# An attention backward loop reordered: two written lists for PE and ACT, six dS buffers, smaller stores and loads

## The chip, the cores and the metric

The kernel runs on 1 core of one Trainium2 chip. The metric is the device time of one execution in microseconds (us). Every kernel was executed several times; the times below are medians. "PE" is the matmul engine, "ACT" the scalar engine, "DVE" the vector engine, "POOL" the general one; "SP" only issues DMA here.

## The reference, cut to what matters

One transformer block with adaptive layer norm, forward and the gradients of all inputs. Sequence 2048, width 512, 32 heads of 16, squared-ReLU MLP of 1792; inputs and outputs are bf16.

```
h   = layernorm(x) * (1 + ca) + sa
qkv = (h @ wqkv) split into q, k, v of 32 heads of 16
p   = softmax(q k^T / 4);   x = x + ga * (p v) @ wo
h   = layernorm(x) * (1 + cb) + sb
x   = x + gb * (relu(h @ w1 + b1)^2 @ w2 + b2)
out, vjp = jax.vjp(block, all inputs);   return out, *vjp(grad_out)
```

Everything below concerns one stage: the gradient of the attention. For each head it recomputes E = exp(scores), forms dS = E * dP, and from E and dS the gradients dV, dK and dQ.

## The kernel before: the parts that matter

The backward loop takes half of the time. Its unit is 4 heads x 128 queries x 512 keys; 4 units are a *block* (16 score matmuls, 8 DVE multiplies), 128 blocks in all, 16 for each group of 4 heads. The softmax's row terms ride in extra rows of q and dO, so that a plain multiply yields dS. For each unit:

```python
PE.matmul(psS, q, k)                        # 4 scores, one PSUM bank each
ACT.activation(E_u[:, hq], psS, Exp)        # 4 exponentials of 128x512
PE.matmul(psD, do, v)                       # 2 pairs of dP, two banks each
DVE.tensor_tensor(dS_u, psD, E_u, mult)     # 2 multiplies of 128x1024
SP.dma_start(dsT[:, qi], dS_u, transpose=True)      # 512 KB
PE.matmul(accVK, qz, dS_u); PE.matmul(accVK, dOs_tok, E_u)  # 2 "quads": dK and dV
```

dQ needs dS transposed. Seven of every eight units are transposed by DMA; the last unit of every second block is transposed on PE in two halves, and ACT evicts each half (`ptT`, 128x1024):

```python
def on_pe(b):
    return b % 2 == 1
def pe_turn(b, half):
    pt = psx.tile([P, 8, P], BF, name="ptT", tag="px")
    for i in range(8):
        PE.transpose(pt[:, i, :], held["dS"][...], identb[:])
    held["turn"] = (dst, pt)          # ACT evicts it in the next step
```

So the loop repeats every **pair of blocks**: one block that carries the two PE transpositions, one plain block. There are 64 pairs. The loop uses eight banks of PSUM, the memory that matmuls write: 4 for dP, 2 for scores, 1 for accVK, and one shared bank `px`, used in turn by some scores, by `ptT` and by the dQ product `dqacc`. E_u and dS_u have four buffers each. One loop over half units emits everything; a score and its exponential are written together:

```python
for j in range(2 * NU + 15):
    for hi in range(2):
        score(u, 2 * pair + hi, shared)      # matmul, then ACT.activation(Exp)
    if "turn" in held: ACT.activation(dst, pt[:], AF.Identity)
    dp_pair(...)                              # dP matmuls, DVE multiply, transposition
    (k_quad if pair == 0 else v_quad)(u - 2)
    if sub in (1, 3) and on_pe(b): pe_turn(b, sub // 2)
    if sub in (5, 6): dq_quad(...)            # dQ of the block before, then its eviction
    ...                                       # loads of the next heads, stores
```

## Time and profile before

| | before |
|---|---|
| median of 3 runs | 2,754.34 us (2,746.58 to 2,755.13) |
| span of the profiled run | 2,744.2 us |
| backward loop | about 1,270 to 2,620 us |
| mean length of a pair of blocks | 20.70 us |

The page's table of groups gives, for each line of the kernel: busy time and mean ns of one, then the engine's idle time before these instructions, and what ended most of it. Two of its lines for the kernel before:

```profile
L1058 DVE TENSOR_TENSOR dS_u<-psD_u,E_u 128x1024 bf16<-128x1024 f32 x1024 | 1196.4, 1217 | 146.8 <-PE psD_u L1056 88.9
...
L1116 PE MATMUL dqacc<-dsT,KS_tok 128*32 128x512 bf16 x2048 | 159.8, 390 | 12.2 <-ACT dsT L1157 12.2
```

DVE needs 1,196 us for its 1,024 multiplies and stands idle 147 us between them: no more than that can be won before DVE is full. The table of stretches for the loop's steady part has busy time and count of each engine, the mean granted clock of PE, the time of the DMA packets as a share of 16 engines' time (1.10 in the line below, so packets overlap), and GB/s:

```profile
core 0: us, PE busy (x) PEld busy (x) DVE busy (x) ACT busy (x) POOL busy (x), PEclk, DMA share, GB/s
1300.00:2560.00 1260.00, 1129.46 (x10664) 384.08 (x10660) 1133.25 (x970) 1180.72 (x2213) 130.98 (x95) 0.98 1.10 191
```

PE, DVE and ACT are each busy 90 to 94%; none is full. The clock of PE is nearly always full (0.98). The list of waits for the same stretch (engine and line, what it waited for, us in total, times, longest) says what separates them:

```profile
DVE dS_u L1058 <- PE psD_u L1056: 70.4, 125, 1.6
PE psS_u L1044 <- ACT E_u L1046: 60.4, 182, 1.1
ACT E_u L1046 <- PE psD_u L1056: 51.1, 80, 4.0
...
DVE dS_u L1058 <- DMA dsT<-dS_u: 16.7, 22, 3.5
```

DVE waits for dP, PE for a score bank that an exponential still holds, ACT for PE, and DVE for a dS buffer that a transposition still reads. The timeline of DVE over a pair (start, duration; in brackets the idle time before and who ended it) shows where: in the pair shown three times, 0.2 to 0.7 us each, around the transposing block.

```profile
2225.83 16.51 DVE L1058 TENSOR_TENSOR dS_u<-psD_u,E_u 128x1024 bf16<-128x1024 f32 x14 [0.61 <-PE psD_u L1056]
2243.03 1.23 DVE L1058 TENSOR_TENSOR dS_u<-psD_u,E_u 128x1024 bf16<-128x1024 f32 x1 [0.69 <-ACT vkb L1101]
2244.49 1.22 DVE L1058 TENSOR_TENSOR dS_u<-psD_u,E_u 128x1024 bf16<-128x1024 f32 x1 [0.23 <-PE psD_u L1056]
2246.40 16.51 DVE L1058 TENSOR_TENSOR dS_u<-psD_u,E_u 128x1024 bf16<-128x1024 f32 x14 [0.69 <-PE psD_u L1056]
```

From 2225.83 to 2246.40 is one pair: 20.57 us.

### The profile page before, as it was taken

To read this page: it belongs to the slowest core of one execution; us is meant where nothing else is said; L and a number is where in the kernel's file an instruction comes from. 1 tells how busy PE (TensorE), PEld (TensorE's weight loads), DVE (VectorE), ACT (ScalarE), POOL (GpSimd) and SP (SyncE) were. 2 spreads that over 40 slices of the span, in tenths; PEclk is the share of its full clock that TensorE was granted. 3 is DMA by queue.
4 is the path that set the end of the run, shared out by engine and by line. 5 is a ranking of instruction groups with operands and counts; after the bars stand their busy time and mean duration, and the time that the engine had idled before them with its cause. 6 is when DMAs were issued, how large, how long until landed. Compare 5 with 4: busy or idle time off the path is not lost.

```text
span 2744.2 us, 48487 instructions
## 1 busy us (share of the span) xinstructions
PE 2383.2 (87%) x18010; PEld 781.8 (28%) x18010; DVE 1763.4 (64%) x2232; ACT 2304.7 (84%) x3537; POOL 379.1 (14%) x378
## 2 busy tenths in 40 slices
PE   6799989888988988586898988988888989888899
PEld 2211123222322222232332333333233232332343
DVE  7101144435345443356988989989999898998973
ACT  4599999999999998202999999999999899998953
POOL 2000010211333133201011110101101011010100
PEclk8655569998998999787999999999999999999999
DMA  9863365346847656786999999999999999999982
GB/s 241 197 177 92 102 147 132 107 116 142 116 83 161 139 95 138 170 226 161 187 179 195 192 194 192 192 195 188 196 193 189 189 190 193 188 188 206 184 247 81
DMA packets 1271906, 459.69 MB, mean 168 GB/s; under 512 B 1152739, under 2 KB 1240807, under 8 KB 1271414
## 3 DMA queue, kind: packets, MB, share of 16 engines
q1 hardware_dynamic: 1254262, 425.42, 77.6%
q0 software_dynamic: 10944, 16.78, 4.2%
q10 hardware_dynamic: 6464, 14.40, 1.9%
q8 instruction: 142, 2.33, 0.3%
q14 instruction: 94, 0.77, 0.1%
HBM read 97.67 MB, written 74.47 MB: 63 GB/s over the span
## 4 chain that ended last, share of the span: by engine, by line
PE 27%; ACT 20%; DMA 4%; DVE 3%; issue 3%; SPq 1%; ACTq 1%; POOL 0%; DVEq 0%; POOLq 0%
ACT E_u L1046 15%; PE psS_u L1044 10%; PE accVK L1098 3%; ACT dsT L1157 3%; PE accVK L1089 3%; DVE dS_u L1058 2%; PE ptT L1079 2%; PE dqacc L1116 2%; PE pdh L1284 2%; PE pwq L1318 2%; DMA dsT<-dS_u 1%; PE psS_x L1044 1%; ACT dqtmp L1126 1%; PE psD_u L1056 1%; DMA part<-p_st 1%
## 5 line engine op out<-in xcount | busy, mean ns | idle before, releaser
L1058 DVE TENSOR_TENSOR dS_u<-psD_u,E_u 128x1024 bf16<-128x1024 f32 x1024 | 1196.4, 1217 | 146.8 <-PE psD_u L1056 88.9
L1046 ACT ACTIVATE E_u<-psS_u 128x512 bf16<-128x512 f32 x1790 | 990.8, 619 | 102.9 <-PE psD_u L1056 53.6
L701 ACT ACTIVATE ET<-psST 128x1024 bf16<-128x1024 f32 x1024 | 944.4, 1299 | 38.7 <-PE psST L699 37.7
L1044 PE MATMUL psS_u<-ik,iq 32*128 32x512 bf16 x1790 | 618.0, 386 | 106.2 <-ACT E_u L1046 64.7
L699 PE MATMUL psST<-qt_sb,kt_sb 32*128 32x512 bf16 x2048 | 408.3, 464 | 64.9 <-ACT ET L701 31.2
L1056 PE MATMUL psD_u<-iv,ido 32*128 32x512 bf16 x2048 | 406.6, 393 | 20.1 <-DMA ido<-dOT_st 14.3
L715 PE MATMUL oacc<-ET,vaug 128*32 128x512 bf16 x2048 | 247.5, 474 | 6.0 <-DVE ostage L719 6.0
L1044 PEld LDWEIGHTS <-iq 32*128 32x128 bf16 x2048 | 121.0, 91 | 342.2 <-issue 315.8
L1089 PE MATMUL accVK<-dS_u,qz 128*32 128x512 bf16 x2048 | 209.6, 398 | 3.0 <-DVE dS_u L1058 0.2
L1098 PE MATMUL accVK<-E_u,dOs_tok 128*16 128x512 bf16 x2048 | 205.4, 391 | 0.0
L699 PEld LDWEIGHTS <-kt_sb 32*128 32x128 bf16 x2048 | 90.0, 94 | 399.7 <-issue 388.6
L1131 POOL TENSOR_TENSOR dQacc<-dQacc,dqtmp 128x512 f32<-128x512 f32 x64 | 81.1, 1268 | 884.6 <-ACT dqtmp L1126 876.8
L1056 PEld LDWEIGHTS <-ido 32*128 32x128 bf16 x2048 | 105.1, 91 | 265.4 <-issue 262.4
L1046 ACT ACTIVATE E_u<-psS_x 128x512 bf16<-128x512 f32 x258 | 160.0, 620 | 14.8 <-PE psS_u L1044 14.6
L1116 PE MATMUL dqacc<-dsT,KS_tok 128*32 128x512 bf16 x2048 | 159.8, 390 | 12.2 <-ACT dsT L1157 12.2
L719 DVE COPY ostage<-oacc 128x512 f32<-128x512 f32 x32 | 22.0, 688 | 229.9 <-PE oacc L715 210.7
L376 DVE COPY part<-pm 128x512 f32<-128x512 f32 (+2 forms) x105 | 64.6, 615 | 150.7 <-PE pm L362 128.1
L1157 ACT ACTIVATE dsT<-ptT 128x1024 bf16<-128x1024 bf16 x128 | 134.4, 1050 | 1.1 <-PE ptT L1079 1.0
L715 PEld LDWEIGHTS <-vaug 128*32 128x32 bf16 x2048 | 54.9, 96 | 163.8 <-issue 163.8
L1044 PE MATMUL psS_x<-ik,iq 32*128 32x512 bf16 x258 | 100.4, 389 | 0.6 <-ACT E_u L1046 0.6
L1079 PE MATMUL ptT<-identb,dS_u 128*128 128x128 bf16 x1024 | 81.3, 224 | 11.6 <-ACT dsT L1157 11.4
L1089 PEld LDWEIGHTS <-qz 128*32 128x32 bf16 x2048 | 55.4, 93 | 123.3 <-issue 121.0
(262 smaller groups left out, 2104.1 us busy)
## 6 DMA issues: line engine op xcount, KB each, us to landing
p_st<-part POOLq DMA_DIRECT2D x36, 256.0 KB, 5.6
kt_sb<-qkT_st SPq DMA_DIRECT2D x128, 64.0 KB
wA<-in_B_w_dram SPq DMA_DIRECT2D x28, 256.0 KB
wB<-w1T_st SPq DMA_DIRECT2D x28, 256.0 KB
dsT<-dS_u SPq DMA_TRANSPOSE x448
wA<-w2T_st SPq DMA_DIRECT2D x21, 256.0 KB
wB<-in_B_w_dram SPq DMA_DIRECT2D x21, 256.0 KB
p_st<-part POOLq DMA_DIRECT2D x27, 192.0 KB, 4.2
```

The source lines that it names most:

```text
L699: PE.matmul(ps[:, hi, :], kt_sb[r:r + 32, kt * P:(kt + 1) * P], qt_sb[r:r + 32, :], start=True, stop=True, tile_position=(r, 0))
L701: ACT.activation(ET[:, 2 * pair:2 * pair + 2, :], ps[:], AF.Exp, scale=SCALE)
L715: PE.matmul(oacc[32 * hq:32 * hq + 32, :], lhsT, ET[:, hq, :], start=(kt == 0), stop=(kt == TT - 1), tile_position=(0, 32 * hq), skip_grou ...
L1044: PE.matmul(psS[:], st["q"][r:r + 32, qt * P:(qt + 1) * P], st["k"][r:r + 32, kc * 512:kc * 512 + 512], start=True, stop=True, tile_positi ...
L1046: ACT.activation(bst[u][0][:, hq, :], psS[:], AF.Exp, scale=SCALE)
L1056: PE.matmul(psD[:, hi, :], st["do"][r:r + 32, qt * P:(qt + 1) * P], st["v"][r:r + 32, kc * 512:kc * 512 + 512], start=True, stop=True, til ...
L1058: DVE.tensor_tensor(dS_u[:, 2 * pair:2 * pair + 2, :], psD[:], E_u[:, 2 * pair:2 * pair + 2, :], ALU.mult)
L1079: PE.transpose(pt[:, i, :], held["dS"][:, 2 * half + i // 4, kt * P:(kt + 1) * P], identb[:])
L1089: PE.matmul(cur["vk"][32 * hq:32 * hq + 32, :], hst[hg]["qz"][:, qt, hq, :], bst[u][1][:, hq, :], start=(qt == 0), stop=False, tile_positi ...
L1098: PE.matmul(acc[32 * hq:32 * hq + DH, :], dOs_tok[:, qt, (hg * 4 + hq) * DH:(hg * 4 + hq + 1) * DH], E_u[:, hq, :], start=False, stop=(qt ...
L1116: PE.matmul(acc[32 * hq:32 * hq + 32, :], KS_tok[:, kc * 4 + kt, h * DH:h * DH + 32], tT[:, :, hq * 4 + kt, :], start=(kt == 0), stop=(kt ...
L1157: ACT.activation(dst, pt[:], AF.Identity)
```

## The change

Its intent is to take the coupling losses out of the loop. The order of PE's and ACT's work is written as two lists, one for the block in which transpositions fall and one for the plain block; scores and exponentials are separate tokens and use three rotating banks A, B, C (C is `px`); dS has six buffers; the dK/dV store and the load of the q tokens are cut into quarters. No arithmetic changes.

```diff
-            yield hs["qs"][:], q_st[hg]
+            for i in range(4):
+                yield hs["qs"][:, 4 * i:4 * i + 4, :], q_st[hg][:, 4 * i:4 * i + 4, :]
...
-                at(j0 + 5 * i, load, to, fro)
+                at(j0 + 4 * i, load, to, fro)
...
+        banks = {"A": "ps0", "B": "ps1", "C": "px"}
...
+            if pair == 0:
+                bst[u][1] = ework.tile([P, 4, 512], BF, name="dS_u", tag="dS_u", bufs=6)
...
-                    if kc == QC - 1: ... at(cur["j"] + 4, load, dVKtP[hg], hst[hg]["vk"][:])
+                    part = slice(kc * 512, (kc + 1) * 512)
+                    at(cur["j"] + 4, load, dVKtP[hg][:, part], hst[hg]["vk"][:, part])
...
+        order_t = (
+            "s0 s1 q s2 e0 e1 D s3 D e2 s4 e3 t1 e4 q T1 D "
+            "s5 s6 e5 t2 e6 s7 T2 e7 D s8 e8 D s9 e9 q q s10 "
+            "s11 e10 D d1 d2 e11 Q q s12 D e12 s13 e13 q s14 D e14 "
+            "s15 q q e15 ").split(), "ABCABBABACABABCA"
+        order_n = (
+            "s0 D s1 q e0 q s2 e1 e2 D s3 s4 q s5 e3 D e4 "
+            "e5 s6 q s7 D s8 e6 e7 d1 e8 s9 D d2 e9 q Q s10 "
+            "s11 e10 D q s12 e11 e12 s13 e13 D q s14 s15 e14 e15 D q ").split(), "CBACBACBABABCABC"
...
-            for j in range(2 * NU + 15):
+            for b in range(NU // 4 + 3):
+                toks, bank = order_t if on_pe(b - 1) else order_n
+                for tok in toks: ...
```

In the lists `s` is a score matmul, `e` an exponential, `D` a pair of dP matmuls with its DVE multiply, `q` one quad for dK or dV, `t` a half of the PE transposition and `T` its eviction, `d` half of the dQ product and `Q` its eviction. The letters after each list are the banks of the 16 scores.

## The prediction

> **What bounds the kernel now.** The backward attention loop runs from 1,270 to 2,620 us, half of the 2,744 us span, and the change touches nothing else. It has 128 blocks (4 units of 4 heads), every second with a transposition on PE. The timeline repeats every pair of blocks: 20.3 to 20.6 us undisturbed, 1,327 us / 64 = 20.7 us on average. No engine is full. From 1,300 to 2,600 us, in the table of stretches, PE is busy about 90%, DVE 90%, ACT 94%, and the DMA engines hold transposes about 92% of the time.
>
> Floors per pair, from start-to-start pitches in the timeline:
> - DVE: 16 multiplies at 1.15 to 1.18 us: 18.4 to 18.9 us.
> - ACT: 32 exponentials at 0.475 us when nothing is missing (0.54 in the usual runs of four), two `ptT` evictions at 0.92, two dQ evictions at 0.475, half a `vkb`: about 18.2 us.[...]
> - PE: counting 0.32 us for each group that can run together (scores and dP in different row groups, quads, transposes), I estimate 18 to 18.5 us.
> - DMA: 7 transposes of 512 KB, 2.35 us each at the best 10 us of the trace, 2.6 to 2.7 over 20 to 30 us, plus loads and stores: 18 to 19 us.
>
> So four resources are near 18.5; about 2 us per pair are coupling losses. The list of waits (1,300 to 2,600) shows DVE idle 130 us: 73 for psD from PE, 17 behind `vkb` on ACT, 17 for dS buffers held by transposes. PE waits 62 for score banks held by exponentials.
>
> **What the change does.** No arithmetic goes. PE issues scores one by one instead of in pairs, three score banks rotate in a fixed list, evictions stand apart from the matmul that they follow, and the transposing block has its own list. ACT gets ahead in the plain block, behind in the other (8.1 and 9.9 us of ACT work against 9.3 of DVE). Six dS buffers (from four) remove most waits for transposes. The quarter stores and loads add 6 issues per head on ACT's queue[...] but split 512 KB bursts.
>
> **How much is critical.** The whole loop. I expect the DVE gaps to fall from 130 to about 50 us, and a pair to take 19.4 to 19.6 us: 64 x 1.2 = about 80 us less. Not more: all four then stand at 94 to 98%, and a faster loop pushes the transposes to their limit.
>
> **Predicted: 2,675 us**, 8 in 10 between 2,635 and 2,725. Faster by over 2%: 0.70; within 2%: 0.28; slower: 0.02.
>
> **What would show it.** Period of a pair of blocks 19.4 to 19.6 us; DVE busy 94 to 95% in the loop; waits of DVE for psD under 40 us and for dS transposes near zero; ACT's waits for PE about halved; durations, start and end unchanged.
>
> **What would make it wrong.** (a) DMA transposes turn out to be the wall: then DVE waits for dS buffers move later but remain, and the pair stays at 20 us or more. (b) A PE blocked at the head of its queue by a psD slot or the shared third bank, since single scores lose their concurrency. (c) More low-clock windows of PE. (d) The list is better than I think, and the pair reaches 18.7 us: 2,620 us.

The forecast's sum: 64 x 1.2, about 80 us off 2,754, hence 2,675. The pitches behind its floors are in the trace of the kernel before: at the least 1.13 us from one multiply to the next, 0.476 us from an exponential and 0.903 us from a `ptT` eviction to ACT's next instruction; and on PE two scores and a dP pair start within 0.02 us of 2227.71, the quad after them at 2228.04, the next scores 0.33 us later.

## The result and the profile after

| | before | after |
|---|---|---|
| median (4 runs each) | 2,753.24 us | 2,716.77 us |
| range | 2,746.58 to 2,755.13 | 2,708.57 to 2,717.54 |
| mean pair of blocks (profiled run) | 20.70 us | 20.21 us |

The ratio is 0.9865, with a 95% interval of 0.984 to 0.989: 1.4% faster, within the 2% that counts as the same. (A ratio here is the mean time of one kernel's runs over that of the other's of the same rounds, so it is not quite the ratio of the medians.) The forecast gain was about 80 us; 36 to 37 came.

First the same two groups, for the kernel after:

```profile
L1061 DVE TENSOR_TENSOR dS_u<-psD_u,E_u 128x1024 bf16<-128x1024 f32 x1024 | 1187.6, 1218 | 122.7 <-PE psS_B L1041 57.9
...
L1119 PE MATMUL dqacc<-dsT,KS_tok 128*32 128x512 bf16 x2048 | 186.3, 474 | 11.8 <-DMA dsT<-dS_u 2.4
```

DVE's idle time fell only from 147 to 123 us, and the largest releaser has another name. The second line is the first clue: the dQ matmuls are the same instructions, yet a mean one went from 390 to 474 ns. The stretch and the waits, in the same columns:

```profile
1300.00:2560.00 1260.00, 1166.90 (x10953) 356.39 (x10949) 1156.09 (x998) 1200.20 (x2275) 136.29 (x99) 0.93 1.14 197
```

```profile
DVE dS_u L1061 <- PE psS_B L1041: 56.4, 41, 1.8
PE psS_C L1041 <- ACT dsT L1189: 28.8, 61, 0.5
ACT dqtmp L1132 <- PE dqacc L1119: 27.3, 37, 0.9
PE ptT L1082 <- ACT dsT L1189: 26.0, 60, 0.4
...
DVE dS_u L1061 <- PE psD_u L1059: 13.1, 22, 1.6
```

The granted clock fell from 0.98 to 0.93. DVE's wait for a transposition is no longer in the list (was 16.7). Its wait for dP seems to fall from 70 to 13 us, but the name misleads: the multiply reads dP and E, not a score, and the score `psS_B` that the list names 41 times runs beside the dP matmuls and ends with them. PE's timeline at one such place, just before DVE starts at 2242.29:

```profile
2241.54 0.60 PE L1059 MATMUL psD_u<-iv,ido 32*128 32x512 bf16 x2
2241.55 0.60 PE L1041 MATMUL psS_B<-ik,iq 32*128 32x512 bf16 x1
```

At each of the 41, dP and the score end within 6 ns of each other, and E had been ready for 0.7 us or more. So dP is what DVE waited for. Counted with all names that the multiply does not read (before, 16.7 us stand under `vkb`), DVE waited for dP about 88 us before and 79 us after: little less, but in another form, with one wait of 1.4 us on average, 41 times, in place of many short ones. And PE waits, once a pair each, for ACT's two evictions of `ptT`. DVE's timeline, first in the most frequent kind of pair, then in the rarer one:

```profile
2221.80 18.91 DVE L1061 TENSOR_TENSOR dS_u<-psD_u,E_u 128x1024 bf16<-128x1024 f32 x16 [1.58 <-PE psS_B L1041]
2242.29 18.91 DVE L1061 TENSOR_TENSOR dS_u<-psD_u,E_u 128x1024 bf16<-128x1024 f32 x16 [1.58 <-PE psS_B L1041]
```

```profile
1841.38 16.47 DVE L1061 TENSOR_TENSOR dS_u<-psD_u,E_u 128x1024 bf16<-128x1024 f32 x14
1858.23 11.46 DVE L1061 TENSOR_TENSOR dS_u<-psD_u,E_u 128x1024 bf16<-128x1024 f32 x10 [0.37 <-PE psD_u L1059]
1870.14 6.10 DVE L1061 TENSOR_TENSOR dS_u<-psD_u,E_u 128x1024 bf16<-128x1024 f32 x5 [0.45 <-PE psD_u L1059]
```

In the first kind all 16 multiplies run without a gap and then DVE stands still for 1.58 us: 20.49 us from start to start. In the second there is no such stop.

Sorting all pairs of the profiled run by whether half-clock time of PE (0.5 us or more) falls into them splits them cleanly. A pair is the interval between the first `ptT` evictions of two successive transposing blocks; 63 can be measured.

| | pairs at full clock | pairs with half clock | half-clock time |
|---|---|---|---|
| before | 55, mean 20.43 us | 8, mean 22.54 us | 48 us |
| after | 13, mean 19.27 us | 50, mean 20.46 us | 176 us |

So the new lists do what was predicted and a little more, 19.27 us, in 13 pairs of 63. In the other 50 PE is throttled (its clock is 0.50 for a time), and the pair is as long as it was before.

The stretches of 3.41 us between the steps of the clock, over one such pair (same columns as above):

```profile
2218.17:2221.58 3.41, 3.35 (x32) 0.86 (x28) 2.02 (x2) 2.58 (x6) 0.10 (x1) 0.50 1.10 211
2221.58:2225.00 3.42, 3.22 (x37) 0.82 (x33) 3.20 (x3) 3.31 (x7) 1.17 (x1) 1.00 1.26 133
2225.00:2228.41 3.41, 3.29 (x35) 0.94 (x37) 3.41 (x4) 3.37 (x8) 0.00 (x0) 1.00 1.07 254
2228.41:2231.82 3.41, 3.35 (x37) 0.96 (x30) 3.41 (x4) 3.38 (x8) 1.27 (x1) 1.00 1.13 211
2231.82:2235.24 3.42, 3.31 (x29) 1.21 (x27) 3.28 (x4) 3.42 (x8) 0.00 (x0) 1.00 1.15 215
2235.24:2238.65 3.41, 2.45 (x25) 0.95 (x24) 3.25 (x4) 3.41 (x7) 0.00 (x0) 1.00 1.15 208
2238.65:2242.06 3.41, 3.35 (x32) 0.86 (x28) 2.02 (x2) 2.20 (x5) 0.10 (x1) 0.50 1.31 159
```

Read the first number after the length (PE busy) and the clock (third from the end). Five stretches have PE busy 3.2 us or more. In the sixth it is busy 2.45 us. In the next one the clock is 0.50. Then it repeats: the half-clock stretches begin 20.48 us apart, which is six of these windows.

What happens in the sixth and seventh stretch is on PE's timeline (count and shape as before; bracket: idle before, releaser):

```profile
2235.05 0.37 PE L1041 MATMUL psS_A<-ik,iq 32*128 32x512 bf16 x1
2235.86 0.61 PE L1082 MATMUL ptT<-identb,dS_u 128*128 128x128 bf16 x8 [0.43 <-ACT dsT L1189]
...
2237.75 0.37 PE L1041 MATMUL psS_C<-ik,iq 32*128 32x512 bf16 x1 [0.47 <-ACT dsT L1189]
...
2238.73 0.58 PE L1041 MATMUL psS_A<-ik,iq 32*128 32x512 bf16 x1
...
2239.28 1.90 PE L1119 MATMUL dqacc<-dsT,KS_tok 128*32 128x512 bf16 x16
```

The second half `t2` of the transposition needs bank C, which ACT is still emptying of the first half: PE waits 0.43 us. Score `s9` needs bank C again: 0.47 us. This is **the hole**. Then a score takes 0.58 us instead of 0.37, exactly where the list has its longest PE work, the 16 dQ matmuls.

Why does that cost so many pairs? Without a throttle, a pair is 19.3 us, which is not a whole number of windows (5.65), so the hole moves through the windows and would meet a bad position only sometimes. With a throttle, a pair is 20.46 us, as long as six windows (20.48). The next hole then falls at the same place in its window, and the throttle comes again. In this account the loop **locks** to the window grid. Of 47 intervals between successive half-clock stretches in 1300 to 2560 us, 40 are six windows long. (The pair of the kernel before, 20.43 us, is also close to six windows; it ran at full clock, so no run shows that this is more than coincidence.)

The grid is in the clock records of the profiled runs of both kernels. The granted clock has two values there, 0.50 and 1.00. In the changed kernel all 150 of its steps, 96 of them between 1300 and 2560 us, lie on one grid of 3.413 us, to within 0.002 us; the 64 steps of the kernel before do as well. The window before the throttle above was not idle: PE was busy for 2.45 of its 3.41 us. What counts instead is taken up below.

### The profile page after: what moved, and what is told of

It is laid out like the page before. It is cut to its first block, busy times and chain, and to the rows that moved or that the text cites. A ratio compares the mean times of both kernels' runs of the same rounds, so it can differ in the third digit from the quotient of the medians.

```text
span 2715.7 us, 48474 instructions
## 1 busy us (share of the span) xinstructions
PE 2387.8 (88%) x17939; PEld 743.3 (27%) x18010; DVE 1754.4 (65%) x2232; ACT 2292.1 (84%) x3537; POOL 379.8 (14%) x378
## 4 chain that ended last, share of the span: by engine, by line
PE 26%; ACT 24%; issue 3%; DMA 3%; DVE 2%; SPq 1%; ACTq 0%; another core or an unknown queue 0%; POOLq 0%; POOL 0%; DVEq 0%
ACT E_u L1047 20%; PE dqacc L1119 6%; PE psS_A L1041 4%; PE accVK L1092 3%; ACT dsT L1189 3%; PE psS_C L1041 2%; PE psS_B L1041 2%; PE pdh L1306 2%; PE pwq L1340 2%; PE accVK L1101 1%; PE psD_u L1059 1%; DMA dsT<-dS_u 1%; ACT dqtmp L1132 1%; DMA part<-p_st 1%; PE pc L362 1%
## 5 line engine op out<-in xcount | busy, mean ns | idle before, releaser
L1047 ACT ACTIVATE E_u<-psS_A 128x512 bf16<-128x512 f32 x768 | 505.8, 659 | 50.2 <-DMA rows_st<-racc 32.3
L1047 ACT ACTIVATE E_u<-psS_B 128x512 bf16<-128x512 f32 x768 | 501.6, 653 | 18.8 <-PE psS_B L1041 14.4
L1059 PE MATMUL psD_u<-iv,ido 32*128 32x512 bf16 x2048 | 427.9, 403 | 14.5 <-DMA ido<-d_st 14.2
L1047 ACT ACTIVATE E_u<-psS_C 128x512 bf16<-128x512 f32 x512 | 332.9, 650 | 1.6 <-DMA dsT<-dS_u 1.0
L1041 PE MATMUL psS_A<-ik,iq 32*128 32x512 bf16 x768 | 308.8, 402 | 13.9 <-ACT E_u L1047 2.5
L1041 PE MATMUL psS_B<-ik,iq 32*128 32x512 bf16 x768 | 310.9, 405 | 10.0 <-ACT E_u L1047 2.2
L1092 PE MATMUL accVK<-dS_u,qz 128*32 128x512 bf16 x2048 | 228.6, 415 | 0.4 <-DVE dS_u L1061 0.2
L1041 PE MATMUL psS_C<-ik,iq 32*128 32x512 bf16 x512 | 194.4, 380 | 33.3 <-ACT dsT L1189 29.3
L1119 PE MATMUL dqacc<-dsT,KS_tok 128*32 128x512 bf16 x2048 | 186.3, 474 | 11.8 <-DMA dsT<-dS_u 2.4
L1189 ACT ACTIVATE dsT<-ptT 128x1024 bf16<-128x1024 bf16 x128 | 148.1, 1157 | 2.8 <-PE ptT L1082 2.7
```

The source lines that it names most:

```text
L1041: PE.matmul(psS[:], st["q"][r:r + 32, qt * P:(qt + 1) * P], st["k"][r:r + 32, kc * 512:kc * 512 + 512], start=True, stop=True, tile_positi ...
L1047: ACT.activation(bst[u][0][:, hq, :], sst.pop((u, hq))[:], AF.Exp, scale=SCALE)
L1059: PE.matmul(psD[:, hi, :], st["do"][r:r + 32, qt * P:(qt + 1) * P], st["v"][r:r + 32, kc * 512:kc * 512 + 512], start=True, stop=True, til ...
L1092: PE.matmul(cur["vk"][32 * hq:32 * hq + 32, :], hst[hg]["qz"][:, qt, hq, :], bst[u][1][:, hq, :], start=(qt == 0), stop=False, tile_positi ...
L1119: PE.matmul(acc[32 * hq:32 * hq + 32, :], KS_tok[:, kc * 4 + kt, h * DH:h * DH + 32], tT[:, :, hq * 4 + kt, :], start=(kt == 0), stop=(kt ...
```

## The experiments

The theory, H: the hole of the transposing block trips the clock, and the loop then locks to the grid. Rivals: R1, the low clock is only a side effect, and the loop is held by DMA transposes or buffers; R2, a PE with any idle time is throttled so often, and nothing in the list matters; R3, the lists are worth little, and the gain comes from the buffers and the smaller transfers.

All runs, with the time of the kernel before on the same chip. "Full" and "half" are the numbers of pairs at full clock and with half clock. "Least busy" is the smallest PE busy time in any 3.41 us of a full-clock pair, and "least work" the smallest array work, in units explained below; both are the median of those pairs, worked out from the records of the one profiled execution (a stretch of half clock that straddles two pairs counts in both). All times are of four runs, and all results are correct except the two marked.

| run | us | before | ratio (95%) | full, median us | half | half-clock us | least busy us | least work |
|---|---|---|---|---|---|---|---|---|
| before | | 2,753.2 | 1 | 55, 20.51 | 8 | 48 | 2.77 | 23.6 |
| after | 2,716.8 | 2,753.2 | 0.987 (0.984–0.989) | 13, 19.31 | 50 | 176 | 2.39 | 21.2 |
| e1_spread | 2,734.1 | 2,750.1 | 0.994 (0.991–0.997) | 1, 19.80 | 62 | 220 | 2.31 | 20.2 |
| e2_fill | 2,706.9 | 2,750.1 | 0.983 (0.980–0.986) | 46, 19.38 | 17 | 70 | 3.17 | 22.8 |
| e7_fill_plain | 2,738.0 | 2,752.0 | 0.994 (0.991–0.997) | 26, 20.23 | 37 | 83 | 2.38 | 21.2 |
| e8_qhole | 2,691.9 | 2,752.0 | 0.979 (0.977–0.981) | 50, 19.31 | 13 | 57 | 2.72 | 22.8 |
| e19_one_small | 2,706.5 | 2,750.3 | 0.985 (0.981–0.989) | 39, 19.31 | 24 | 113 | 3.02 | 21.7 |
| e20_one_full | 2,702.5 | 2,750.3 | 0.983 (0.980–0.986) | 50, 19.31 | 13 | 82 | 2.87 | 22.8 |
| e3_ds4 | 2,733.3 | 2,750.1 | 0.994 (0.991–0.997) | 21, 19.43 | 42 | 171 | 2.48 | 21.2 |
| e4_whole | 2,712.4 | 2,752.0 | 0.986 (0.983–0.989) | 23 | 40 | 150 | | 21.2 |
| e6_before_ds6_q | 2,741.2 | 2,750.1 | 0.996 (0.994–0.998) | 58, 20.51 | 5 | 45 | 2.77 | 23.6 |
| e9_fill_spaced | 2,702.0 | 2,752.0 | 0.982 (0.980–0.983) | 47, 19.38 | 16 | 71 | | 22.8 |
| e10_fill_pool | 2,724.7 | 2,752.0 | 0.990 (0.988–0.992) | 45, 19.38 | 18 | 94 | | |
| e12_qhole_spaced | 2,697.3 | 2,752.0 | 0.980 (0.978–0.982) | 45 | 18 | 82 | | |
| e13_qhole_pooldq | 2,694.9 | 2,752.0 | 0.980 (0.978–0.982) | 49 | 14 | 70 | | |
| e14_pooldq_ds8 | 2,693.1 | 2,750.6 | 0.980 (0.978–0.982) | 46, 19.31 | 17 | 71 | | |
| e15_qhole_ds8 | 2,696.5 | 2,750.6 | 0.980 (0.979–0.982) | 45 | 18 | 65 | | |
| e11_qhole_noloads (wrong result) | 2,666.4 | 2,752.0 | 0.969 (0.967–0.970) | 54, 19.29 | 9 | 34 | 2.73 | 22.8 |
| e17_after_noloads (wrong result) | 2,711.0 | 2,750.6 | 0.986 (0.985–0.988) | 17, 19.31 | 46 | 154 | | 21.1 |
| e18_after_again | 2,718.2 | 2,750.6 | 0.988 (0.984–0.992) | 14, 19.32 | 49 | 164 | | |

### Move the hole, fill it, or fill elsewhere

**e1_spread** pulls the two transposition halves apart, so that the second does not wait for the eviction of the first.

```diff
-            "s5 s6 e5 t2 e6 s7 T2 e7 D s8 e8 D s9 e9 q q s10 "
+            "s5 s6 e5 e6 s7 e7 D s8 e8 t2 D s9 e9 T2 q q s10 "
-            "s15 q q e15 ").split(), "ABCABBABACABABCA"
+            "s15 q q e15 ").split(), "ABCABBABABABABCA"
```

> The changed kernel with the second PE transposition of a block (t2 and its eviction T2) moved behind s8/e9, so that the two evictions stand about 3.3 us apart instead of 1.86; nothing else differs but the banks of s9 to s11. Theory (clock): in the changed kernel both transpositions and the waits around them fall into one 3.41 us clock window in which PE does little else, the next window is granted at half clock, and the pair of blocks is held at 20.46 us instead of the 19.27 us of its undisturbed pairs (50 of 63). Then spreading removes most of the low-clock windows (under 60 us in the loop, from 176), the median pair falls to 19.3 to 19.6 us and the time to 2,655 to 2,685 us. Rival (the DMA transposes or the order of the engines' queues set 20.4 us): no fewer than 2,705 us, pairs still 20.2 us or more.

This was a miss, and a useful one. The time rose to 2,734 us, inside the rival's range, and half-clock time rose to 220 us where under 60 was expected. PE's timeline of that run shows that the hole had only moved: the bank that is now short is B, held by exponentials that stand behind the eviction `T1`.

```profile
2022.39 0.37 PE L1041 MATMUL psS_B<-ik,iq 32*128 32x512 bf16 x1 [0.92 <-ACT E_u L1047]
```

The stretches of the same run, cut at the clock's steps, show the same signature as before, 2.39 us busy and then a low clock:

```profile
2020.71:2024.12 3.41, 2.39 (x27) 0.91 (x27) 3.39 (x3) 3.18 (x6) 0.00 (x0) 1.00 1.12 225
2024.12:2027.53 3.41, 3.29 (x35) 0.95 (x32) 2.45 (x3) 2.98 (x5) 0.00 (x0) 0.50 1.11 203
```

62 of 63 pairs were throttled; 57 of 58 intervals between half-clock stretches are six windows. The locked pair is 20.51 us although its only undisturbed one was 19.80, not 19.3: the length that it locks to is the grid's, not the list's. My repair was wrong, and the theory gained, though one undisturbed pair is little to judge by.

**e2_fill** leaves the list alone and puts two dummy matmuls ahead of the scores `s6` and `s8` of the transposing block; the score overwrites their bank. It adds work to PE and takes none away.

```diff
+            for _ in range(fill):
+                PE.matmul(psS[:], KS_tok[:, 0, 0:P], KS_tok[:, 1, 0:512], start=True, stop=True)
-                        score(4 * b + i // 4, i % 4, bank[i])
+                        score(4 * b + i // 4, i % 4, bank[i], 2 if on_pe(b - 1) and i in (6, 8) else 0)
```

> The changed kernel with four useless full-array matmuls of 512 columns added per pair of blocks: two into the score bank just before s6 and two just before s8 of the transposing block, overwritten by the score that follows. No wait, order or buffer differs. Theory (clock): the windows that precede a throttle have PE busy 2.46 of 3.41 us; the filler lifts them by up to 0.85 us, the low-clock windows go (under 60 us of 176), the pair falls to 19.3 to 19.7 us and the kernel gets faster by doing more work, 2,655 to 2,690 us. Rivals (DMA wall, queue order): PE has more to do and nothing is freed, so the time stays at 2,715 or rises up to 2,760 us.

(Its 0.85 us for four dummies agrees with the changed kernel's trace: there matmuls of 512 columns on 128 rows by 128 columns start 0.216 us apart at full clock, the median of 1,084.)

With more work on PE the kernel is about 10 us faster than the changed one (2,706.9 against 2,716.8), half-clock time falls from 176 to 70 us, and throttled pairs from 50 to 17; the undisturbed pair is 19.38 us, as expected. The time missed its range (2,655 to 2,690 us), half-clock time its limit of 60 us, and the 95% interval of the ratio overlaps that of the changed kernel, so the clock is the stronger evidence here. R1 and R2 as they stand do not expect it. The same stretch as above has the clock back at 0.97:

```profile
1300.00:2560.00 1260.00, 1204.12 (x11324) 366.08 (x11320) 1162.22 (x1008) 1214.07 (x2297) 137.46 (x100) 0.97 1.16 198
```

**e7_fill_plain** is the control: the same dummies in the plain block, where there is no hole.

```diff
-                        score(4 * b + i // 4, i % 4, bank[i])
+                        score(4 * b + i // 4, i % 4, bank[i], 2 if not on_pe(b - 1) and i in (6, 8) else 0)
```

> Control to the filler run: the same four useless matmuls, but before s6 and s8 of the block without a PE transposition, where PE has no idle stretch. Clock theory: the window with the hole is untouched, low clock stays at 150 us or more in the loop, median pair 20.4 us or more, time 2,710 to 2,740 us. Rival (the filler of the earlier run helped by delaying PE in some lucky way, or by any extra PE activity): 2,695 to 2,710 us here too.

The time is at the upper edge of what was expected, 2,738 us. The half-clock time was a miss: it fell to 83 us. The control disturbed more than it should: the plain block has no room on PE, and the undisturbed pair grew to 20.23 us. The hole itself stayed (2.38 us at the least). The half-clock stretches now mostly come 12, 18 or 24 windows apart (13 of 19 intervals), hence every second, third or fourth pair: a low spot without the tight lock (the table's 37 half-clock pairs come from 21 stretches, 17 of which straddle two pairs). This suggests that the lock, not the low spot alone, is what makes every pair slow. That the pair's new length is the reason is an argument; no run varied the length alone.

This run also contradicts the theory as it stood. 17 of its 20 half-clock stretches do not follow the hole at all, but stretches in which PE is busy nearly all the time. One of them, from the table of stretches of this run:

```profile
1624.60:1628.01 3.41, 3.27 (x27) 0.95 (x24) 3.06 (x4) 3.41 (x8) 0.21 (x1) 1.00 1.02 224
1628.01:1631.43 3.42, 3.42 (x28) 1.75 (x30) 2.88 (x3) 3.00 (x6) 0.00 (x0) 0.50 0.82 156
```

PE is busy for 3.27 us in the first, and it is throttled in the second. PE's timeline shows scores there that run alone: those at 1624.66, 1625.63 and 1625.96 have nothing beside them for 0.30 to 0.33 us each, where others start together with a dP pair. What that means is taken up after the next run.

**e8_qhole** fills the hole with useful work. One quad is moved from before `T1` to before `t2`, another to before `s9`.

```diff
-            "s0 s1 q s2 e0 e1 D s3 D e2 s4 e3 t1 e4 q T1 D "
-            "s5 s6 e5 t2 e6 s7 T2 e7 D s8 e8 D s9 e9 q q s10 "
+            "s0 s1 q s2 e0 e1 D s3 D e2 s4 e3 t1 e4 T1 D "
+            "s5 s6 e5 q t2 e6 s7 T2 e7 D s8 e8 D q s9 e9 q s10 "
```

> The changed kernel with no work added: in the transposing block two quads of matmuls are moved into the two stretches where PE waits for an eviction of ptT (one q from before T1 to just before t2, one q from after e9 to just before s9). Clock theory: the same PE work spread more evenly lifts the hole's window by about 0.6 of 3.41 us, the lock at 20.46 us goes for most pairs: low clock under 90 us in the loop, median pair 19.2 to 19.6 us, time 2,680 to 2,705 us. Rival: PE's order at this place does not matter, 2,710 to 2,725 us.

This is the best correct version: 2,691.9 us, 25 us under the changed kernel and 2.1% under the kernel before (interval 1.9 to 2.3%). It has 50 undisturbed pairs of 19.31 us where the changed list had 13 of the same 19.31. So the two moved tokens do not shorten the pair; they only keep PE's clock, 0.98 in the stretch of this run:

```profile
1300.00:2560.00 1260.00, 1156.90 (x11199) 380.04 (x11197) 1170.49 (x1014) 1212.16 (x2302) 141.49 (x103) 0.98 1.17 200
```

PE's timeline of e8_qhole shows what was left of the wait for bank C:

```profile
2153.51 0.61 PE L1082 MATMUL ptT<-identb,dS_u 128*128 128x128 bf16 x8 [0.20 <-ACT dsT L1189]
```

0.20 us instead of 0.43, and the second wait, before `psS_C`, is nearly gone (1.1 us in the whole stretch, was 28.8). A wait of 0.3 us a pair for bank A (20.1 us in all) has come in.

### What the clock counts

The stretch of e7_fill_plain suggests that the clock depends on the work of PE's array, not on its busy time. The largest tile in these records is 128 rows by 128 columns, taken here as the whole array; a score's is 32*128, a quarter of that, and yet PE is "busy" while it runs alone. I took as unit a quarter of the array for 512 columns of moving data. Then a score matmul, a dP matmul, and each matmul of a quad (128 rows by 32 or 16 columns) is one unit, a transposition (the whole array, 128 columns) also one, and a full dummy four. All windows of the grid that ran at full clock between 1300 and 2560 us, of the 18 profiled runs other than the two that follow below, 6,063 in number, 412 of them followed by half clock, split so (a matmul's units are spread evenly over its record):

| array work in the window | windows | followed by half clock |
|---|---|---|
| under 23 units | 315 | 303 |
| 23 to 24 | 202 | 103 |
| 24 and more | 5,546 | 6 |

The best single limit, 23.57 units, sorts 61 windows wrongly; the best limit on PE's busy time, 2.50 us, 135, and 61 throttles follow windows that were busy for 3 us or more. The limit depends on the weights. With transpositions at 0 in place of 1 the best limit errs 380 times, with 0.5 some 114, with 1.25 167. That the clock counts matmuls whatever their size fits worse: with a full dummy counted as one, not four, the best limit for the five runs with full dummies errs 51 times in place of 10. But the unit isn't strictly area: a quad's matmul on 16 columns fills an eighth of the array, and counted so the best limit errs some 114 times. The weights were fitted after the fact on few values, though, so two more runs tested the idea by intervention.

**e19_one_small** is the changed kernel with one dummy in place of e2_fill's two ahead of `s6` and `s8`, on 32 rows by 32 columns, a sixteenth of the array; **e20_one_full** has the same dummies on the whole array. That both take the same time on PE was assumed: at full clock the changed kernel's records of 512-column matmuls have medians of 0.38 us on 32*128 and on 128*128, and 0.38 to 0.39 us on 128*16 and 128*32; none is on 32*32.

```diff
 # e20_one_full
+                PE.matmul(psS[:], KS_tok[:, 0, 0:P], KS_tok[:, 1, 0:512], start=True, stop=True)
 # e19_one_small
+                PE.matmul(psS[0:32, :], KS_tok[r:r + 32, 0, 0:32], KS_tok[r:r + 32, 1, 0:512],
+                          start=True, stop=True, tile_position=(r, 0))
 # both
+                        score(..., 1 if on_pe(b - 1) and i in (6, 8) else 0)
```

(The rival: that the clock follows PE's busy time, for which the first ranges stand.)

> One dummy matmul of 32 rows x 32 columns of the array (1/16 of it) ahead of each of the scores s6 and s8 of the transposing block, in the changed kernel. It fills PE's idle time in the hole as well as a full one does, but adds almost no work: counted in quarter arrays times 512 columns (a score 1, a quad's matmul 1, a 128x128 transposition 1), the hole's least 3.41 us hold 21.2 units in the changed kernel, 21.7 here; PE busy there rises from 2.39 to 2.8 or more. [...]this unlocks the loop as e2_fill did: at most 22 pairs of 63 with half clock, half-clock time at most 90 us, 2,700 to 2,712 us. If it counts array work with a limit near 23.5 units (theory), the hole still trips it: 35 pairs or more, half-clock time 130 us or more, 2,712 to 2,740 us.

> The same two dummies, on the whole array (128 rows x 128 columns): the same PE time, 16 times the array work each (4 units each, so the hole's stretch has about 29 in place of 21.2). Both ideas, busy time and array work, expect this to unlock: at most 22 pairs of 63 with half clock, half-clock time at most 90 us, 2,698 to 2,712 us. If it stays locked, both fall and two dummies are too few.

e20_one_full did what both ideas expected: 13 throttled pairs, 2,702.5 us. (Its trace lacks the matmul records of one of the two dummies in each pair, though their weight loads are there; e7_fill_plain, e9_fill_spaced and e10_fill_pool lack one in four. What the table says of them is worked out without these records; put back, they change hardly any of the counts above.) e19_one_small landed between the two expectations: 24 pairs and 113 us at half clock miss both, and 2,706.5 us lies in the range of busy time. It does speak against busy time, as e7_fill_plain did: its hole is filled, and windows busy for 3.17 us were still followed by half clock, as its stretches show:

```profile
1552.67:1556.08 3.41, 3.17 (x29) 1.12 (x29) 3.25 (x3) 3.41 (x7) 0.00 (x0) 1.00 1.00 112
1556.08:1559.50 3.42, 3.42 (x32) 0.74 (x24) 2.45 (x2) 2.20 (x5) 0.00 (x0) 0.50 1.28 209
```

But it does not confirm area exactly. With a sixteenth (a quarter unit) for each dummy, the border between windows with and without a throttle lies near 21.8 units in this run. If such a dummy counts as a whole unit, like a score, the border is at about 23.3, near that of the other runs, and the best limit errs twice in place of 7 times. So a 32 by 32 tile seems to count for more than its area, as the tile of 16 columns does. That reading was made after the run and is not tested. Between e19_one_small and e20_one_full the times do not differ clearly (the intervals overlap). What stands, as a fit and not as a rule: work done in the window, in these units, separates the windows best, with a border near 23.5 units, about 37% of the 64 units that the whole array could do in 3.41 us (an estimate: at half clock four dQ groups of four units each take 1.90 us in the changed kernel's timeline, the last some 0.60 us, so they start 0.43 us apart; at full clock that is 0.22, about 16 groups in a window; the 0.216 us between matmuls on 128*128 says the same).

In this light the hole is poor in work because PE waits 0.43 and 0.47 us for bank C within one window, between transpositions and scores that fill little of the array. The kernel before has its own lowest spot at 23.6 units, just at the border; the changed kernel's is at 21.2, e1_spread's at 20.2. e2_fill, e8_qhole and e20_one_full have theirs at 22.8, somewhat under it and yet not locked; a window must be cut by the grid just so to be that low, and that they miss it mostly is argued, not shown.

### Which part of the change is worth what

**e3_ds4** is the changed kernel with four dS buffers again.

```diff
-                bst[u][1] = ework.tile([P, 4, 512], BF, name="dS_u", tag="dS_u", bufs=6)
+                bst[u][1] = ework.tile([P, 4, 512], BF, name="dS_u", tag="dS_u")
```

> The changed kernel with four dS buffers as before, own lists and quarters kept. If the six buffers matter (DMA latency close to the wall), DVE waits for transposes come back: 30 us or more, 2,735 to 2,770 us. Clock theory: the period is held at 20.46 us by the clock, so a small delay is swallowed by the lock or knocks it out; 2,710 to 2,740 us, low clock still over 100 us in the loop.

This is the range of the clock theory, and 2 us under that of the buffers. It loses 15 to 17 us (2,733.3 against 2,716.8 and 2,718.2), and the wait for transpositions is back, in the list of waits of this run:

```profile
DVE dS_u L1061 <- DMA dsT<-dS_u: 24.2, 34, 2.9
```

So the six buffers seem to carry nearly half of the change's gain of 36 us. The undisturbed pair is 19.43 us even with four.

**e6_before_ds6_q** is the kernel before with six buffers and the quarters, but without the lists: the edits of the first diff above, except for the lists and banks.

> The kernel before with only the buffer and DMA parts of the change: six dS buffers, dK/dV stores and q token loads in quarters, loads every 4 steps; old order of PE and ACT work. It tells what the lists alone are worth. Before, DVE waited 17 us for dS buffers, and some 8 pairs of blocks around the loads took 21.2 to 22.2 us in place of 20.4: I expect 10 to 25 us less than before, 2,728 to 2,744 us. Steady pairs stay at 20.2 to 20.6 us, full clock.

It gains 0.4% (about 11 us by the ratio). Its undisturbed pair stays at 20.51 us, that of the kernel before. So R3 is half right about the time that arrived, and wrong about the pair: only the lists shorten the undisturbed pair, by over 1 us, and it is their gain that the clock takes back.

**e4_whole** is the changed kernel with whole loads and stores again.

```diff
-            for i in range(4):
-                yield hs["qs"][:, 4 * i:4 * i + 4, :], q_st[hg][:, 4 * i:4 * i + 4, :]
+            yield hs["qs"][:], q_st[hg]
-                at(j0 + 4 * i, load, to, fro)
+                at(j0 + 5 * i, load, to, fro)
...     # and one dVKtP store per head group in place of four
```

> The changed kernel with the stores of dK/dV and the q token load whole again (512 and 256 KB, loads every 5 steps as before); lists and six buffers kept. If splitting the bursts matters, the pairs around a head's turn get longer and the time rises by 5 to 20 us over the changed kernel (ratio to before 0.988 to 0.994, against 0.9865). If it does not, 0.985 to 0.988; the lock at 20.46 us may hide it, as a pair held by the clock leaves the DMA engines slack.

Its ratio, 0.9861, is the changed kernel's, 0.9865. The quarters are worth nothing that these runs can see.

### What stands behind the lock

With the lock gone in e8_qhole, 63 pairs of 19.3 us would make some 30 us less than it takes (its mean pair is 19.78 us: 63 x 0.47). One or two pairs in each group of heads last 22 to 24 us, where the dQ of the finished heads is stored and the next heads are loaded. DVE's timeline of e8_qhole at such a turn, and a cut from its chain of waits (start, duration, what):

```profile
1781.20 1.23 DVE L1061 TENSOR_TENSOR dS_u<-psD_u,E_u 128x1024 bf16<-128x1024 f32 x1 [2.61 <-ACT E_u L1047]
1784.23 2.36 DVE L1061 TENSOR_TENSOR dS_u<-psD_u,E_u 128x1024 bf16<-128x1024 f32 x2 [1.80 <-PE psS_B L1041]
```

```profile
1773.82 6.38 DMA dsT<-dS_u
...
1780.22 0.31 ACTq L1018
1780.58 0.61 ACT E_u L1047
```

ACT's queue is about to issue a small transfer (line 1018 is the helper that issues loads and stores on ACT), stands still for 2.75 us until a transposition, in flight for 6.38 us, has landed, and only then goes on with exponentials. DVE then loses 4.4 us. In e2_fill the same holds for a dQ store: its chain has a transposition in flight from 2111.72 for 6.23 us, and the store's issue at 2117.98. A shared semaphore would explain it, and the changed kernel's trace shows one: from 1300 to 2560 us its 647 issues, 441 of SP's and 206 of ACT's, name the same eight semaphore numbers, each begins only after the recorded landings of the transfer before it with its number, and a dQ store at 1796.29 begins 0.02 us after a transposition with its number has landed. That an issue waits for its number's last user is my reading of these records; what it costs was not tested. Several attempts to use it:

**e9_fill_spaced** (on e2_fill) and **e12_qhole_spaced** (on e8_qhole) stretch the dQ stores and start the loads later.

```diff
-                at(j0 + 4 * i, load, to, fro)
-            at(j0 + 40, spread_qz, hg)
+                at(j0 + 14 + 4 * i, load, to, fro)
+            at(j0 + 54, spread_qz, hg)
-                    at(cur["j"] + 6 + hq, load, dQc[...], st["dq"][...])
+                    at(cur["j"] + 6 + 3 * hq, load, dQc[...], st["dq"][...])
```

> The filler kernel with the ACT-issued DMAs of a head pulled apart: the four dQ stores every third step instead of every step, the loads of the next head starting 14 steps later, so that they no longer fall together. In the filler run one pair per head took 23 to 24 us, in which ACT stood before the issue of a dQ store that waits for a semaphore last used by a DMA transposition. If these waits are what keeps the filler kernel from its 19.33 us pairs: pairs above 22 us go, 2,680 to 2,697 us. If the DMA engines are simply full there, the stall moves elsewhere: 2,700 to 2,710 us.

> The qhole list with the dQ stores every third step and the loads 14 steps later. The same edit took 5 us off the filler kernel. Expected 2,680 to 2,690 us; if nothing, 2,690 to 2,696.

**e10_fill_pool** (on e2_fill) issues these loads and stores from POOL, **e13_qhole_pooldq** (on e8_qhole) only the dQ stores.

```diff
         def load(to, fro):
-            ACT.dma_start(out=to, in_=fro)
+            POOL.dma_start(out=to, in_=fro)
```

> The filler kernel with all loads and stores of the loop issued by POOL, which is idle 86% of the time, instead of ACT: the wait for a shared DMA semaphore then holds POOL, not ACT. If ACT's stalls at the issue cost what the 23 to 24 us pairs show (7 heads, about 4 us each, and low-clock windows after them): 2,665 to 2,692 us. If the DMA engines are full, DVE waits for dS buffers instead and the time stays within 2,698 to 2,712 us.

> The qhole list with only the four dQ stores of a head issued by POOL; loads and dK/dV stores stay on ACT. In the qhole run ACT stands 2 to 3 us per head before the issue of a dQ store, waiting for a semaphore last used by a transposition in flight. If that wait is the cost of the turn: 2,665 to 2,682 us. If the DMA engines are behind anyway, DVE waits for dS buffers instead, as when POOL issued everything: 2,688 to 2,705 us.

**e14_pooldq_ds8** and **e15_qhole_ds8** are e13_qhole_pooldq and e8_qhole with `bufs=8` for dS.

> The qhole list with the dQ stores issued by POOL and eight dS buffers in place of six. If the DMA engines are only late in a burst at a head's turn, two more buffers (about 4.6 us of DVE work) carry DVE over it: DVE waits for transpositions near zero, time 2,665 to 2,682 us. If they are full on average at 19.3 us per pair, the backlog eats the buffers too: 2,685 to 2,700 us.

> The qhole list with eight dS buffers, dQ stores on ACT as before. As DVE hardly waited for dS buffers in the qhole run (1.3 us in the loop) and ACT's wait before a dQ store is untouched: 2,685 to 2,696 us, no gain.

None of them helped beyond noise; e10_fill_pool lies above both of its ranges, e12_qhole_spaced and e15_qhole_ds8 end about 1 us above theirs. Spacing gave 0.1% on e2_fill (0.9827 to 0.9816, intervals overlap) and nothing on e8_qhole. Taking the issues off ACT moved the wait instead of removing it: in e10_fill_pool, which is slower than e2_fill, DVE itself now waits for the transpositions, says its list of waits:

```profile
DVE dS_u L1063 <- DMA dsT<-dS_u: 31.3, 19, 3.7
```

and two more buffers (e14_pooldq_ds8, e15_qhole_ds8) did not help either: their medians lie within 5 us of e8_qhole's. This suggests that the place of the wait is not its cause, and that the transfers themselves are late. The remaining suspect is the total of DMA work at the turn.

**e11_qhole_noloads** and **e17_after_noloads** take the loads of the heads after the second group away, in e8_qhole and in the changed kernel. The result is wrong (relative error 4.73 in the third output of e11_qhole_noloads); the loop does the same work on stale data.

```diff
-            for i, (to, fro) in enumerate(loads):
+            for i, (to, fro) in enumerate(loads if hg == 1 else []):
```

> WRONG RESULT ON PURPOSE: the list of the qhole run, with the loads of heads 2 to 7 left out (heads use stale operands; same instructions, all stores kept). In the qhole run 50 pairs of blocks ran undisturbed at 19.29 us and the rest, mostly one or two per head, at 21.7 us on average. If the loads of the next head, together with the transposes, overfill the DMA engines (the wall the prediction named as its first risk), these pairs fall to 19.3 to 20 us and the time to 2,655 to 2,670 us. If the pairs are long for another reason (the dQ stores and their waits, the order at a head's turn), 2,680 to 2,692 us.

> WRONG RESULT ON PURPOSE: the changed kernel, its own list, with the loads of heads 2 to 7 left out. Separates the two causes. If the clock holds the pair at 20.46 us by itself, freeing the DMA engines does not free the loop: most pairs stay at 20.4 to 20.5 us, low clock over 140 us, 2,695 to 2,715 us, although the qhole list without loads took 2,666 us. If the DMA load is what makes PE late and so trips the clock: 2,660 to 2,680 us.

**e18_after_again** is the changed kernel on the chip of e17_after_noloads, for comparison.

> The changed kernel itself once more, beside the others on the same chip: ratio to before 0.984 to 0.989, pairs mostly at 20.4 to 20.5 us with a low-clock window each.

| median us | with loads | without loads | difference |
|---|---|---|---|
| changed list | 2,718.2 | 2,711.0 | 7 |
| list of e8_qhole | 2,691.9 | 2,666.4 | 26 |
| difference | 26 | 45 | |

(The two rows are of different calls; the runs of the kernel before differ by under 2 us between them.) The same loads cost 7 us under the lock and 26 us without it. And without the loads the changed list, which locks, takes 45 us more than the list of e8_qhole. Of the loss against the undisturbed pair, the lock hides a part that is DMA's: removing either one uncovers the other. That e17_after_noloads still locks is seen in its stretches, with the same hole before the throttle:

```profile
2079.65:2093.31 13.66, 13.15 (x129) 3.85 (x125) 12.80 (x12) 13.54 (x28) 2.54 (x2) 1.00 1.09 184
2093.31:2096.72 3.41, 2.45 (x27) 1.07 (x27) 3.32 (x3) 3.41 (x7) 0.00 (x0) 1.00 1.00 225
2096.72:2100.13 3.41, 3.41 (x32) 0.73 (x29) 2.45 (x2) 2.58 (x7) 2.77 (x1) 0.50 1.07 201
```

That decides against R1 as well: taking the DMA work away leaves the half clock where it was (154 against 164 us). Why the transfers at a turn are late, bandwidth or the shared semaphores, is not separated: in e8_qhole at least 8 packets are in flight 97.4% of the time from 1300 to 2560 us (before: 92.6%), worked out from the packet records, which speaks for a nearly full queue but does not prove a wall.

## Why the prediction was right or wrong

- **The undisturbed pair: right.** 19.4 to 19.6 us was predicted, 19.27 measured (20.43 before). The floors were read well enough: DVE's 16 multiplies take 18.91 us in the timeline, and 0.4 us per pair remain.
- **DVE's waits: half right.** For transpositions 16.7 us to none listed, as predicted. For dP under 40 us was predicted; the list says 13, but with the waits that it puts under other names it is about 79, against 88 before. The many short waits went, and the throttle put one long one in their place.
- **ACT's waits for PE: half right.** The exponentials' waits for PE fell from 63 to 16 us (dP and scores together), but the evictions of dQ now wait 27.3 and 8.7 us (before: 7.1 and 0.6), because the dQ matmuls are the ones that fall into the half clock.
- **DVE busy 94 to 95%: wrong**, 91.8% (1,156 of 1,260 us). Gaps of about 50 us in the loop: wrong, 104.
- **Durations unchanged: wrong.** The matmuls behind the hole take 0.58 to 0.61 us against 0.37 to 0.39.
- **The average pair: wrong, and this is the step that failed.** The sum multiplied the saving of an undisturbed pair by 64 ("64 x 1.2 = about 80 us less") and put nothing on the risk it named under (c), "more low-clock windows of PE". 50 of 63 pairs have one; 63 x (20.21 - 19.27) = 59 us are lost by that, in the profiled run. The floors for PE were counted at full clock.
- **Risk (b) named the cause, but not its price.** "The shared third bank" does block PE, by 0.43 and 0.47 us a pair (26 and 29 us in the list). Their direct cost is small: the 13 undisturbed pairs have the same waits, and DVE loses some 0.4 us in such a pair in all. They cost through the clock. That single scores lose their concurrency is seen in the stretch of e7_fill_plain, and matters there through the clock too.
- **Risk (a), the DMA wall,** exists at the heads' turns, where it costs 26 us once the lock is gone, and 7 us in the changed kernel.
- **The time.** 2,675 us was predicted and 2,716.8 measured; it lies in the range of 2,635 to 2,725, near its upper end, only because the range was wide: 36 to 37 us came of a forecast 80, and 0.70 had been put on a gain of more than 2%.

Shown by runs: the two lengths of a pair and the clock in them; that adding work at the hole (e2_fill, e20_one_full) or moving work there (e8_qhole) removes most throttles without making the undisturbed pair shorter, while the loads don't cause them; and that busy time does not decide the clock (e7_fill_plain, e19_one_small). Fitted to the records: the border near 23.5 units of array work. Argued from the spacing of the stretches, and supported by e1_spread and e7_fill_plain: the lock to six windows. Pairs and clock come from one profiled execution of each kernel. Open: how narrow tiles are counted, and whether transfers at the turns are late for bandwidth or for shared semaphores.

## What to carry to other kernels

When a schedule is packed tighter, look at how much array work each stretch between possible steps of the clock (here 3.41 us) holds, not only at how busy PE is in total: here one spot where two waits, of 0.43 and 0.47 us, met scores on a quarter of the array was followed by half clock in the loop's longest PE work, and a loop whose throttled pair was six windows long repeated it in 50 of 63 pairs. Sort a loop's periods by the granted clock in them, and if they fall into two lengths, move one small piece of work into the poor stretch. Multiply a saving by the number of iterations only after asking what the faster iteration triggers, and expect the next limit (here DMA at the turns) to take back part of what the repair wins.
